# Other seeds for the planner that orders an adaLN transformer block on one core

## The chip, the cores and the metric

One core of one Trainium2 chip runs the whole kernel. The metric is device time in microseconds (us), the median of three runs. Five engines work beside each other: TensorE (PE in the profile, its weight loads PEld), VectorE (DVE), ScalarE (ACT), GpSimd (POOL) and SyncE (SP, which issues nearly all DMAs).

## What is computed

One transformer block of 2048 tokens, 512 channels and 32 heads of 16 channels, with six modulation vectors made from a condition `c`:

```python
x = A_x
mod = (_silu(c) @ w_mod).reshape(c.shape[0], 6, 1, -1)
sa, ca, ga, sb, cb, gb = ...
h = _layernorm(x, axis=-1) * (1 + ca) + sa
x = x + ga * _A_ref(h, A_wqkv, A_wo)        # softmax attention, 32 heads, head width 16
h = _layernorm(x, axis=-1) * (1 + cb) + sb
x = x + gb * _B_ref(h, B_w1, B_b1, B_w2, B_b2)   # 512 -> 1376, gelu, -> 512
return x
```

The softmax over 32 heads of 2048 by 2048 scores is by far the largest part: 134 million exponentials.

## The kernel before

**Tiling.** The queries are cut into four blocks of 512. A run is four heads against one block of queries (in the last block half the queries of eight heads); there are 32 runs, `runs`. A run goes over 16 tiles of 128 keys. A tile of keys is four units of 128 keys by 512 scores, one for each head or half.

**Two ways to take the exponential.** A unit's scores are made by a matmul that uses 32 of the array's 128 rows (`qk`, L824), so that up to four of them run beside each other. On the ACT way (`qk_a`, `ex` at L873) two or three units (`SPAN = (3, 2)`) lie in one PSUM tile `st`, and one ACTIVATE with Exp turns them into `pt`. On the DVE way (`qk_d`, L914, and `shifts`, L929) the score is turned into the bits of a bf16 number by adding a constant (`ph`, four instructions for a tile of keys, one for each unit), and four shifted copies (`sh`, four instructions for a tile of keys) are weighted and averaged. Each product with V (`pv_op`, L962, output `od`) is four matmuls that use all 128 rows: one such group for a tile of keys on the ACT way, five on the DVE way (one with `ph`, four with `sh`). Tiles 2, 6, 10 and 14 of each run (`DKS`; in the first run tile 14 alone) may go either way, up to 31 x 4 + 1 = 125 in all: DVE takes them when it is free for them, and `next_tile` gives those to ACT that DVE has not taken by the time ACT has nothing else of that run.

**Around them** stand the layer norms, the q, k and v projections, the gates (`mod_columns` and `gate_bc`, made after the first and the fourth run), the products with Wo, W1 and W2 for each finished block (`block_tail`), and a tail for the last half block (`last_half`).

**The planner.** All order is fixed when the kernel is built. `Plan` holds a list of work that could be next on each engine and a model of its own of when each engine, tile and buffer is free. `step` asks `pick` for each engine's best candidate and commits the one that starts first. `pick` keeps the candidates that start within a slack of the first and takes the one with the smallest sum of a priority (`dyn`) and `spread`:

```python
def spread(self, o):
    seed = SEEDS[min(int(self.now // 12.5), len(SEEDS) - 1)]
    x = (o.seq * 2654435761 ^ seed * 2246822519) & 0xFFFFFFFF
    x = ((x ^ x >> 15) * 2246822519) & 0xFFFFFFFF
    return SPREAD * (seed % 4) * ((x ^ x >> 13) & 1023) / 1024.0
```

So each stretch of 12.5 us of plan time has a seed. The seed makes a number between 0 and 1 out of each piece of work's serial number, and its remainder by 4 sets how far that number can move a choice: nothing for 0, up to 0.3, 0.6 or 0.9 for 1, 2 and 3 (`SPREAD = 0.3`). The priorities that it is added to lie 0.05 to some units apart: a candidate in PE's present mode has 0.5 less, a second score matmul for an ACT that is already supplied costs 2.2, for a DVE 7.

The planner also keeps a record of PE work (`done`), in which a matmul that uses a part of the rows counts for that part, and holds it against two bounds, `FILL` (1.6 us) and `HEAT` (1.3 us) within `WIN` (3.4 us): work that can wait is held back while the record is full enough, and where it runs short, `heat` adds matmuls on zeros (L433, L438, L449) or doubles a `pv` (`o.extra`, L953). A piece of `mod_columns` (`mod_mm`, four matmuls with one column each, L585, and for every second piece one on zeros, L588) is put down there with 0.36 us.

Of the kernel before, what the change touches and what calls it, by code (L numbers as in the profile page):

```python
# [59 lines left out]
AL = 0.21  # L60
FILL = 1.6
SPREAD = 0.3
SEEDS = (0, 0, 755, 57, 694, 691, 918, 614, 162, 803, 681, 731, 49, 608, 441, 365, 202, 75, 571, 0, 661, 578, 62, 537, 834, 873, 727, 838, 707, 887, 118, 138, 118, 945, 551, 781, 821, 803, 995, 659, 439, 0, 251, 929, 855, 38, 992, 86, 978, 926, 309, 0, 0, 16, 0, 0, 829, 892, 0, 736, 454, 0, 0, 0, 0, 0)
HEAT = 1.3


# [39 lines left out]
class Plan:  # L106
# [51 lines left out]
# [5 lines that stand above are left out]
# [1292 lines left out]
```

## Time and profile before

| | us |
|---|---|
| median of three runs (lowest, highest) | 792.81 (791.49, 794.11) |
| the profiled execution's own time | 788.26 |
| its span, first to last instruction | 786.5 |
| ScalarE's 631 exponentials, busy | 715.7 |
| PE busy on scores for ACT, and for DVE | 249.3, 162.8 |

The mean granted TensorE clock of the profiled execution is 0.991. Busy times are sums over the whole span; for one engine they cover overlapping instructions once. PE's busy time counts waits inside its pipeline, so it is not array use.

The two halves of the page's second part that matter are the rows by slices of the span: the clock row is 9, full speed, in every slice but the seventh, where it is 7.

### The profile page before, as it was taken

To read this page: it belongs to the slowest core of one execution; us is meant where nothing else is said; L and a number is where in the kernel's file an instruction comes from. 1 tells how busy PE (TensorE), PEld (TensorE's weight loads), DVE (VectorE), ACT (ScalarE), POOL (GpSimd) and SP (SyncE) were. 2 spreads that over 40 slices of the span, in tenths; PEclk is the share of its full clock that TensorE was granted. 3 is DMA by queue.
4 is the path that set the end of the run, shared out by engine and by line. 5 is a ranking of instruction groups with operands and counts; after the bars stand their busy time and mean duration, and the time that the engine had idled before them with its cause. 6 is when DMAs were issued, how large, how long until landed. Compare 5 with 4: busy or idle time off the path is not lost.

```text
span 786.5 us, 20298 instructions
## 1 busy us (share of the span) xinstructions
PE 736.1 (94%) x8240; PEld 272.4 (35%) x8240; DVE 732.9 (93%) x1277; ACT 757.6 (96%) x685; POOL 127.9 (16%) x279
## 2 busy tenths in 40 slices
PE   8899989999999888999999999989999999999998
PEld 3333322233332222223323232222233444344454
DVE  6879797999999999999999999998999999999994
ACT  4999998999999999999999999999999999999994
POOL 6520304103224310110001000010000200010100
PEclk9999997999999999999999999999999999999999
DMA  7033001000020101000101100011011001100010
GB/s 215 30 98 129 18 24 43 25 6 17 23 73 24 25 16 50 19 15 13 42 20 29 30 18 17 20 26 39 23 45 29 18 18 26 37 24 18 25 44 28
DMA packets 39072, 28.21 MB, mean 36 GB/s; under 512 B 17957, under 2 KB 34374, under 8 KB 38978
## 3 DMA queue, kind: packets, MB, share of 16 engines
q1 hardware_dynamic: 38970, 26.91, 12.3%
q8 instruction: 64, 1.05, 0.6%
q14 instruction: 30, 0.25, 0.1%
q10 hardware_dynamic: 8, 0.00, 0.0%
HBM read 21.30 MB, written 2.61 MB: 30 GB/s over the span
## 4 chain that ended last, share of the span: by engine, by line
ACT 51%; PE 24%; issue 11%; DVE 10%; DMA 2%; SPq 1%; POOL 1%; POOLq 0%; ACTq 0%; DVEq 0%
ACT pt L873 49%; PE od L962 8%; PE st L824 7%; DVE ph L914 3%; DVE sh L929 2%; PE ax L824 2%; PE ax L1125 2%; DVE ln_s L609 1%; DMA dc<-dn 1%; ACT g L1204 1%; PE ax L1185 1%; PE ax L703 1%; PE ax L433 1%; DMA Wo<-in_A_wo_dram 1%; PE t L1125 1%
## 5 line engine op out<-in xcount | busy, mean ns | idle before, releaser
L873 ACT ACTIVATE pt<-st 128x1536 bf16<-128x1536 f32 (+1 forms) x631 | 715.7, 1351 | 6.1 <-PE st L824 4.0
L914 DVE TENSOR_SCALAR ph<-ax 128x512 int16<-128x512 f32 x472 | 309.7, 681 | 15.2 <-PE ax L824 12.8
L929 DVE TENSOR_SCALAR sh<-ph 128x2048 int16<-128x2048 int16 x472 | 310.7, 691 | 3.3 <-PE od L962 2.7
L824 PE MATMUL st<-qm,kT 32*128 32x512 bf16 x1576 | 249.3, 385 | 28.5 <-ACT pt L873 23.1
L962 PE MATMUL od<-sh,VX 128*32 128x512 bf16 (+1 forms) x2384 | 169.8, 341 | 5.1 <-DVE sh L929 4.5
L824 PEld LDWEIGHTS <-kT 32*128 32x128 bf16 x2048 | 84.0, 91 | 245.6 <-issue 235.5
L824 PE MATMUL ax<-qm,kT 32*128 32x512 bf16 x472 | 162.8, 382 | 4.2 <-DVE ph L914 2.3
L962 PE MATMUL od<-pt,VEB 128*32 128x512 bf16 (+1 forms) x1964 | 150.1, 343 | 0.4 <-DVE OD L987 0.2
L962 PEld LDWEIGHTS <-VEB 128*32 128x32 bf16 x2560 | 62.3, 96 | 79.0 <-issue 66.8
L962 PEld LDWEIGHTS <-VX 128*32 128x32 bf16 x2384 | 59.4, 95 | 77.3 <-issue 66.6
L1014 POOL TENSOR_TENSOR OT<-OD,RB 128x256 bf16<-128x256 f32 x38 | 27.8, 742 | 289.5 <-DVE sh L929 155.8
L962 PE MATMUL od<-ph,VEB 128*32 128x512 bf16 (+1 forms) x596 | 45.8, 338 | 0.3 <-DVE OD L987 0.2
L1014 POOL TENSOR_TENSOR OS<-OD,RB 128x256 bf16<-128x256 f32 x24 | 17.3, 728 | 171.2 <-DVE sh L929 123.7
L1185 PE MATMUL ax<-blk,W 128*128 128x512 bf16 (+1 forms) x164 | 42.7, 362 | 0.3
L703 PE MATMUL ax<-blk,w 128*128 128x512 bf16 x124 | 36.6, 382 | 1.8 <-DVE blk L628 1.5
L758 POOL TENSOR_SCALAR VX<-VEB 128x128 bf16<-128x128 bf16 x64 | 24.6, 386 | 52.7 <-DVE VEB L635 49.3
L1125 PE MATMUL ax<-w,g 128*128 128x512 bf16 x112 | 30.7, 381 | 0.8 <-DVE ph L914 0.6
L1195 DVE TENSOR_SCALAR g<-ax,b1c 128x512 bf16<-128x512 f32 (+1 forms) x41 | 28.1, 689 | 0.5 <-PE ax L1185 0.4
L609 DVE BATCH_NORM_STATS2 ln_s<-xb 128x6 f32<-128x512 bf16 x32 | 21.7, 678 | 1.6 <-DMA xb<-in_A_x_dram 1.5
L1125 PEld LDWEIGHTS <-g 128*128 128x128 bf16 x176 | 14.3, 97 | 22.8 <-issue 11.6
L987 DVE COPY OD<-od 128x512 f32<-128x512 f32 x31 | 21.1, 682 | 0.9 <-PE od L962 0.4
L1185 PEld LDWEIGHTS <-W 128*128 128x128 bf16 x176 | 13.4, 97 | 22.0 <-issue 16.6
(110 smaller groups left out, 371.4 us busy)
## 6 DMA issues: line engine op xcount, KB each, us to landing
RB<-rn SPq DMA_DIRECT2D x124, 64.0 KB
xb<-in_A_x_dram SPq DMA_DIRECT2D x8, 512.0 KB
out_dram<-o SPq DMA_DIRECT2D x16, 128.0 KB
qm<-qs SPq DMA_DIRECT2D x120, 16.0 KB
W<-in_B_w_dram SPq DMA_DIRECT2D x1, 1376.0 KB
w<-in_A_wqkv_dram SPq DMA_DIRECT2D x3, 384.0 KB
blk<-in_w_mod_dram SPq DMA_DIRECT2D x2, 512.0 KB
g<-in_w_mod_dram SPq DMA_DIRECT2D x2, 512.0 KB
```

Of the source, the lines that this page charges most:

```text
L609: nc.vector.bn_stats(out=st6, in_=src)
L703: return chain([(lambda ps, j=j: nc.tensor.matmul(out=ps[:, 0:QB], lhsT=w.tile[:, j, cc * P:(cc + 1) * P], rhs=o_h[b].tile[:, j, :], start ...
L758: nc.gpsimd.tensor_scalar(out=v_cols(VX[(t, ph)])[:, 8 * cc:8 * cc + 8, 0:16], in0=v_cols(v_tile(t, 0))[:, 8 * cc:8 * cc + 8, 0:16], scala ...
L824: nc.tensor.matmul(out=o.tile[:, k * QB:(k + 1) * QB], lhsT=kT[cc][kb][rows, ko * P:(ko + 1) * P], rhs=qm.tile[rows, par, :] if hb is None ...
L873: nc.scalar.activation(out=e.tile[:, 0:len(got) * QB], in_=o.tile[:, 0:len(got) * QB], func=ACT.Exp, scale=ESC)
L914: nc.vector.tensor_scalar(out=ph.tile[:, o.row * QB:(o.row + 1) * QB], in0=o.tile, scalar1=PH_B, scalar2=0.0, op0=ALU.add, op1=ALU.max)
L929: sh = op("DVE", lambda o, j=j: nc.vector.tensor_scalar(out=o.tile, in0=first.tile, scalar1=PH_SH[j], scalar2=None, op0=ALU.add), 0.6, es, ...
L962: nc.tensor.matmul(out=o_od[r].tile[32 * i:32 * i + 32, n * HB:n * HB + w], lhsT=v_tile(kt, ph)[:, c0:c0 + 32], rhs=got[i][:, at:at + w], ...
L1014: two = beside(lambda c: nc.gpsimd.tensor_tensor(out=OT.tile[:, c], in0=OD.tile[:, c], in1=o5.tile[:, c], op=ALU.mult), (OT,), (OD, o5))
L1125: nc.tensor.matmul(out=ps, lhsT=g[:, f, col:col + P], rhs=rhs, start=(f == 0), stop=(f == NF - 1))
L1185: mm = chain([(lambda ps, f=f, j=j: nc.tensor.matmul(out=ps[:, 0:N], lhsT=W1[:, j, f * P:(f + 1) * P], rhs=h.tile[:, j, 0:N], start=(j == ...
L1195: ev.append(op("DVE", lambda o, f=f, mm=mm: nc.vector.tensor_scalar(out=g.tile[:, f, 0:N], in0=mm.tile[:, 0:N], scalar1=b1c[:, f:f + 1], s ...
```

## The change

One constant, the tuple of 66 seeds. Its first three entries, and so the plan up to 37.5 us of plan time, are the same.

```diff
-SEEDS = (0, 0, 755, 57, 694, 691, 918, 614, 162, 803, 681, 731, 49, 608, 441, 365, 202, 75, 571, 0, 661, 578, 62, 537, 834, 873, 727, 838, 707, 887, 118, 138, 118, 945, 551, 781, 821, 803, 995, 659, 439, 0, 251, 929, 855, 38, 992, 86, 978, 926, 309, 0, 0, 16, 0, 0, 829, 892, 0, 736, 454, 0, 0, 0, 0, 0)
+SEEDS = (0, 0, 755, 5, 531, 719, 518, 847, 0, 618, 302, 387, 314, 297, 323, 63, 661, 775, 827, 615, 0, 331, 0, 619, 409, 891, 627, 607, 511, 251, 875, 267, 66, 589, 745, 78, 323, 767, 603, 547, 399, 0, 59, 231, 254, 891, 299, 903, 259, 790, 0, 0, 957, 0, 0, 140, 0, 0, 0, 928, 0, 0, 0, 0, 0, 0)
```

In words, the new seeds were chosen with a penalty on short stretches of the plan that hold little TensorE work. The penalty was used in choosing them and is not in the kernel. Of the old seeds 19, 14, 17 and 16 have the remainders 0, 1, 2 and 3 by 4; of the new ones 21, 7, 8 and 30. No operation, tile, buffer or shape is edited; which engine takes a tile of `DKS`, and how many matmuls on zeros are added, follow from the plan and may differ.

## The prediction

> **What bounds the kernel now.** I read the page first: busy times, the chain of waits, the costliest groups.
>
> ```profile
> span 786.5 us, 20298 instructions
> ...
> PE 736.1 (94%) x8240; PEld 272.4 (35%) x8240; DVE 732.9 (93%) x1277; ACT 757.6 (96%) x685; POOL 127.9 (16%) x279
> ...
> ACT 51%; PE 24%; issue 11%; DVE 10%; DMA 2%; SPq 1%; POOL 1%; POOLq 0%; ACTq 0%; DVEq 0%
> ...
> L873 ACT ACTIVATE pt<-st 128x1536 bf16<-128x1536 f32 (+1 forms) x631 | 715.7, 1351 | 6.1 <-PE st L824 4.0
> L914 DVE TENSOR_SCALAR ph<-ax 128x512 int16<-128x512 f32 x472 | 309.7, 681 | 15.2 <-PE ax L824 12.8
> L929 DVE TENSOR_SCALAR sh<-ph 128x2048 int16<-128x2048 int16 x472 | 310.7, 691 | 3.3 <-PE od L962 2.7
> ```
>
> ACT is busiest and half of the chain is its exponentials, though DVE and PE are close. The 472 `ph` are 118 tiles of keys on the DVE way (four units each), of 125 that may go there; the other 2048 - 472 = 1576 units are ACT's, at 715.7 / 1576 = 0.454 us each.
>
> Then the busy times by stretch, cut where ACT's exponentials become continuous (41.53) and where they end (763.45). After the time in the stretch, the columns are PE, PEld, DVE, ACT and POOL busy with their instruction counts, granted clock, DMA share, GB/s.
>
> ```profile
> 0.00:41.53 41.53, 35.35 (x296) 16.78 (x296) 29.44 (x70) 28.61 (x31) 24.12 (x105) 1.00 0.39 117
> 41.53:763.45 721.92, 681.58 (x7781) 243.95 (x7779) 692.99 (x1183) 717.15 (x623) 102.21 (x170) 0.99 0.12 32
> 763.45:786.50 23.05, 19.13 (x167) 11.62 (x166) 10.43 (x24) 11.86 (x32) 1.60 (x4) 1.00 0.08 25
> ```
>
> In the middle ACT idles for 721.92 - 717.15 = 4.77 us. So an order can win there by two things alone: those 4.77 us, and a different number of units for ACT. ACT's order of time says where the idle lies (start, length, group; idle before it in brackets):
>
> ```profile
> 129.98 2.54 ACT L873 ACTIVATE pt<-st 128x1024 bf16<-128x1024 f32 x2 [0.87 <-PE ax L824]
> 132.68 1.02 ACT L873 ACTIVATE pt<-st 128x1024 bf16<-128x1024 f32 x1 [0.16 <-PE st L824]
> 134.20 1.45 ACT L873 ACTIVATE pt<-st 128x1536 bf16<-128x1536 f32 x1 [0.50 <-PE st L824]
> 136.47 4.62 ACT L873 ACTIVATE pt<-st 128x1024 bf16<-128x1024 f32 x4 [0.82 <-PE ax L824]
> ...
> 264.03 55.61 ACT L873 ACTIVATE pt<-st 128x1024 bf16<-128x1024 f32 x49 [0.84 <-PE st L824]
> 320.67 10.49 ACT L873 ACTIVATE pt<-st 128x1536 bf16<-128x1536 f32 x9 [1.03 <-PE st L824]
> ```
>
> 2.35 us between 129 and 137, 0.84 us at 263, 1.03 us at 320. All wait for scores from PE. Last, short stretches around these places, same columns:
>
> ```profile
> 122.51:125.93 3.42, 2.55 (x32) 1.08 (x28) 3.39 (x7) 3.42 (x4) 1.52 (x3) 1.00 0.29 87
> 125.93:136.17 10.24, 9.91 (x71) 2.55 (x70) 6.63 (x16) 8.13 (x7) 4.26 (x6) 0.50 0.10 28
> 313.66:317.07 3.41, 2.58 (x27) 0.73 (x23) 3.41 (x7) 3.41 (x4) 1.24 (x2) 1.00 0.02 4
> 317.07:320.49 3.42, 3.42 (x25) 0.61 (x24) 2.22 (x4) 2.57 (x3) 0.17 (x1) 0.50 0.08 18
> 259.05:262.46 3.41, 2.60 (x29) 0.75 (x26) 2.15 (x6) 3.41 (x4) 0.82 (x2) 1.00 0.09 16
> 511.60:515.01 3.41, 2.67 (x36) 0.90 (x28) 3.11 (x7) 3.41 (x4) 0.00 (x0) 1.00 0.08 17
> ```
>
> From 125.93 to 136.17 and from 317.07 to 320.49 the granted clock is 0.50: two falls, 10.24 and 3.41 us long and 191.15 us apart, which are 3, 1 and 56.0 times 3.413. So I cut the middle into pieces of 3.413 us on that grid. The two pieces just ahead of the falls are the two in which PE was busy least, 2.55 and 2.58 us; the next, at 259.05, has 2.60 and no fall follows. While the clock is down PE cannot feed both ways and ACT waits 2.35 + 1.03 = 3.38 us.
>
> [...]
>
> **The change part by part.** *Start.* Three seeds stay, so the plan to 37.5 us is the same: 0.
>
> *The falls.* If no piece of the middle is as poor in PE work as those two, ACT gets back 2.35 + 1.03 = 3.38 us. Bounds: nothing, if the poor stretches move instead of going, and 3.38 us; another execution may cut the stretches elsewhere, and 4.55 us lie between the profiled execution's 788.26 and the median 792.81, two to four falls at 1.03 to 2.35 us each. Whether they are falls this profile cannot say, so they only widen the range downward. I take 3.38 us, since what it needs is small: 2.65 us of PE work per piece in place of 2.55. The gap at 263 follows a DVE that waited for a transfer; I leave it.
>
> *The split between ACT and DVE.* A tile moved from DVE to ACT costs ACT 4 x 0.454 = 1.82 us and frees DVE of 4 x 0.681 + 4 x 0.691 = 5.49 us; moved the other way it gives the same. In the middle DVE idles for 721.92 - 692.99 = 28.9 us, room for 5.3 tiles, within the 7 that it leaves to ACT: at best 5.3 x 1.82 = 9.6 us less. On the other side, an order that doubles DVE's idle time loses as much, 9.6 us. No row says which way, so I take 0.
>
> *Matmuls on zeros.* L433, L438, L449 and L953 together are 9.4 + 4.4 + 8.8 + 3.2 = 25.8 us of PE's busy time. A plan with fewer poor stretches may want fewer; one that adds as many again would still lie in PE's 721.92 - 681.58 = 40.3 us of idle middle. Taken 0. If that cover is gone where ACT needs scores, it shows as ACT waiting for `st`, at 0.2 to 1 us a place as above.
>
> *DMAs and the end.* Each DMA is issued as before; those of the normalisation (`RB`, `dn`, `dc`) and of `qm` change places on SP. POOL, which waits for them, is 16% busy; what is late next is `od` after `OD`, and PE waited 0.2 us for that. Behind the last exponential lie 23.05 us in which seeds are 0 in both plans but for one (454 to 0): 0, with 1 us either way.
>
> *Sum.* Against the profiled execution: 786.5 - 3.4 = 783.1 of span, 788.26 - 3.38 = 784.9 of time. Its own time lies 4.55 us under the median of the runs shown, so the same step from the median gives 792.81 - 3.38 = **789.4 us**.
>
> [...]
>
> **The rivals.**
>
> *Fewer tiles for DVE.* Seeds that spread PE work evenly are not those that give ACT least work. For it: 30 of the new seeds against 16 have the remainder that moves choices most, by up to 0.9, which outweighs the 0.5 that keeps PE in its mode; and DVE's largest wait is already for scores (12.8 us for `ax`). Against it: the same disorder may fill DVE's 28.9 idle us. Four tiles fewer make 4 x 1.82 = 7.3 us, less 3.38: 792.81 + 3.9 = 796.7. Where the falls go, it makes the kernel slower beyond 0.3% from (3.38 + 2.38) / 1.82 = 3.2 tiles; where they stay, from 1.3 tiles.
>
> *More tiles for DVE.* Two: 789.4 - 3.6 = 785.8.
>
> *The planner does not see the first fall.* The piece ahead of it holds the columns of `mod_mm`:
>
> ```profile
> L585 PE MATMUL ax<-sc,g 128*128 128x1 bf16 x32 | 1.8, 168 | 0.0
> L588 PE MATMUL ax<-warm 128*128 128x384 bf16 x4 | 1.8, 442 | 0.0
> ```
>
> The planner puts eight pieces down at 0.36 us, 2.9 us of PE work; the L585 rows hold 1.8 us for 32 columns of one element. A penalty on the planner's account finds nothing poor there. Then the second fall alone goes: 792.81 - 1.03 = 791.8. Against it: any other order shifts what stands beside those columns.
>
> *Falls have nothing to do with these orders.* 2.58 fell and 2.60 did not, which is thin. Then nothing changes: 792.8.
>
> **How the numbers follow.** A measurement of this kernel can tell about 0.3% from no change, 2.4 us: 790.4 and 795.2 are the bounds. Chances: falls gone with the split about as it was 0.34 (789.4; own range 787 to 790.4), more tiles for DVE 0.10, first fall unseen 0.18, nothing to do with it 0.05, fewer tiles or new falls of its own 0.33. So faster 0.34 + 0.10 = 0.44, same 0.18 + 0.05 = 0.23, slower 0.33. The range runs from 784.5, which holds two tiles more and leaves out most of the four-fall gain, to 797.5, four tiles fewer and a little; one in ten is left outside at each end.
>
> **What would show it.** Right: granted clock 1.00 in every stretch between 41 and 763, ACT idle there under 1.5 us, `ph` 472 give or take 4, span near 783. Wrong by the split: `ph` at 456 or fewer and more than 631 exponentials. Wrong by the planner's account: a fall still at the columns of L585 after the first run. Wrong altogether: as many falls as before, at other places, or ACT waiting for `st` at full clock.

## The result and the profile after

| | us, median | runs (lowest to highest) |
|---|---|---|
| before: the three runs shown with the prediction and two more | 792.81 | 5 (791.49 to 794.11) |
| changed | 786.26 | 5 (784.57 to 788.06) |
| before, three later jobs together | 789.71 | 93 (784.37 to 797.17) |
| changed, two of those jobs | 787.64 and 787.05 | 12 and 12 (784.48 to 789.12) |

The first comparison gives a ratio of 0.9918 (95% interval 0.9894 to 0.9942), the two repeats 0.997 (0.9945 to 0.9996) and 0.996 (0.9936 to 0.9984). The kernel is faster in all three, though the interval of the first repeat ends just under 1. How much faster was a question of its own, since the first five runs of before lay high: 28 of the 93 later ones reach 791.49.

The page of the changed kernel, the same lines as before:

```profile
span 786.2 us, 20185 instructions
...
PE 727.6 (93%) x8136; PEld 274.3 (35%) x8215; DVE 732.8 (93%) x1277; ACT 757.6 (96%) x685; POOL 128.4 (16%) x279
...
ACT 45%; PE 28%; DVE 13%; issue 10%; DMA 2%; POOL 1%; SPq 0%; POOLq 0%; DVEq 0%; ACTq 0%
...
L873 ACT ACTIVATE pt<-st 128x1536 bf16<-128x1536 f32 (+1 forms) x631 | 715.5, 1364 | 5.5 <-PE st L824 4.6
L914 DVE TENSOR_SCALAR ph<-ax 128x512 int16<-128x512 f32 x472 | 309.5, 681 | 13.4 <-PE ax L824 11.5
L929 DVE TENSOR_SCALAR sh<-ph 128x2048 int16<-128x2048 int16 x472 | 311.4, 690 | 1.7 <-PE od L962 1.1
```

The split between ACT and DVE is the same to the instruction: 631 exponentials, 472 `ph`, 472 `sh`, and the busy times agree within 1 us. The span of this execution, 786.2, is within 0.3 us of the profiled one of before, 786.5. So the page alone would say that nothing happened. (PE's 8136 matmuls against 8240 are mostly records that the trace lacks: L703 has 95 of 124 here, and 124 in a later profile of the changed kernel. The rest is a difference of the plans: L449, groups of four matmuls on zeros, has 64 in place of 88.)

Where the profiled execution lost time, by stretches. Columns as in the prediction: PE, PEld, DVE, ACT and POOL busy, granted clock, DMA share, GB/s. The last line is a piece that no fall follows.

```profile
31.47:34.88 3.41, 2.39 (x18) 0.98 (x17) 2.62 (x3) 2.89 (x5) 2.09 (x18) 1.00 0.00 0
34.88:41.71 6.83, 6.47 (x41) 3.05 (x40) 2.96 (x6) 4.91 (x4) 0.29 (x1) 0.50 0.07 17
304.53:307.94 3.41, 2.36 (x28) 0.73 (x28) 3.41 (x7) 3.41 (x4) 0.00 (x0) 1.00 0.27 55
307.95:311.36 3.41, 3.41 (x30) 0.70 (x23) 2.40 (x4) 2.78 (x3) 0.67 (x1) 0.50 0.13 32
...
615.13:618.55 3.42, 2.26 (x42) 1.19 (x42) 2.82 (x6) 3.42 (x4) 2.17 (x2) 1.00 0.00 0
```

The two falls at 126 and 317 us are gone, and two others are there: 6.83 us at 34.88, in a part of the program that both kernels share, and 3.41 us at 307.95. ACT's order of time shows where it idles for them (idle before each group in brackets):

```profile
34.84 1.02 ACT L873 ACTIVATE pt<-st 128x1024 bf16<-128x1024 f32 x1 [0.52 <-PE st L824]
36.18 1.45 ACT L873 ACTIVATE pt<-st 128x1536 bf16<-128x1536 f32 x1 [0.32 <-PE st L824]
37.81 1.02 ACT L873 ACTIVATE pt<-st 128x1024 bf16<-128x1024 f32 x1 [0.17 <-PE st L824]
39.74 1.45 ACT L873 ACTIVATE pt<-st 128x1536 bf16<-128x1536 f32 x1 [0.91 <-PE st L824]
42.02 1.02 ACT L873 ACTIVATE pt<-st 128x1024 bf16<-128x1024 f32 x1 [0.82 <-PE st L824]
...
43.40 3.73 ACT L873 ACTIVATE pt<-st 128x1536 bf16<-128x1536 f32 x3
...
310.28 1.02 ACT L873 ACTIVATE pt<-st 128x1024 bf16<-128x1024 f32 x1 [0.57 <-PE st L824]
311.70 97.28 ACT L873 ACTIVATE pt<-st 128x1536 bf16<-128x1536 f32 x86 [0.40 <-PE ax L824]
```

2.74 us around the early fall, 0.97 us around the other. The first 0.52 us of the 2.74 are not the fall's. A later profile of the changed kernel, which has no early fall, shows them too:

```profile
35.68 5.54 ACT L873 ACTIVATE pt<-st 128x1024 bf16<-128x1024 f32 x5 [0.52 <-PE st L824]
...
41.53 4.70 ACT L873 ACTIVATE pt<-st 128x1536 bf16<-128x1536 f32 x4
```

From the first of these five exponentials to the one behind them ACT takes 43.40 - 34.84 = 8.56 us with the fall and 41.53 - 35.68 = 5.85 us without it. So the early fall costs 2.7 us. Idle time alone gives 2.2, since exponentials that do not wait overlap a little: the five have 5.96 us of their own and take 5.54 together.

The same kernel falls near 35 us in one execution and not in another, so one profile of each kernel is one draw. Every run lists its span and mean granted clock, and those are what to compare.

### The profile page after: what moved, and what is told of

It reads as the page before. It is cut to its first block, busy times and chain, and to the rows that moved or that the text cites. A ratio compares the mean times of both kernels' runs of the same rounds, so it can differ in the third digit from the quotient of the medians.

```text
span 786.2 us, 20185 instructions
## 1 busy us (share of the span) xinstructions
PE 727.6 (93%) x8136; PEld 274.3 (35%) x8215; DVE 732.8 (93%) x1277; ACT 757.6 (96%) x685; POOL 128.4 (16%) x279
## 4 chain that ended last, share of the span: by engine, by line
ACT 45%; PE 28%; DVE 13%; issue 10%; DMA 2%; POOL 1%; SPq 0%; POOLq 0%; DVEq 0%; ACTq 0%
ACT pt L873 43%; PE od L962 9%; PE st L824 8%; DVE sh L929 5%; DVE ph L914 4%; PE ax L824 2%; PE ax L1185 2%; PE ax L1125 2%; ACT g L1204 1%; DVE ln_s L609 1%; PE ax L703 1%; DMA blk<-in_w_mod_dram 1%; PE t L1125 1%; PE ax L742 1%; PE ax L1119 1%
## 5 line engine op out<-in xcount | busy, mean ns | idle before, releaser
L873 ACT ACTIVATE pt<-st 128x1536 bf16<-128x1536 f32 (+1 forms) x631 | 715.5, 1364 | 5.5 <-PE st L824 4.6
L824 PE MATMUL st<-qm,kT 32*128 32x512 bf16 x1576 | 248.4, 384 | 34.4 <-ACT pt L873 27.7
L962 PE MATMUL od<-sh,VX 128*32 128x512 bf16 (+1 forms) x2384 | 173.9, 341 | 4.0 <-DVE sh L929 2.7
L824 PEld LDWEIGHTS <-kT 32*128 32x128 bf16 x2048 | 84.2, 91 | 241.2 <-issue 231.9
L824 PE MATMUL ax<-qm,kT 32*128 32x512 bf16 x472 | 163.9, 379 | 3.9 <-DVE ph L914 2.2
L962 PE MATMUL od<-pt,VEB 128*32 128x512 bf16 (+1 forms) x1964 | 151.0, 342 | 0.1
L962 PEld LDWEIGHTS <-VEB 128*32 128x32 bf16 x2560 | 63.0, 95 | 80.2 <-issue 68.7
L962 PEld LDWEIGHTS <-VX 128*32 128x32 bf16 x2384 | 61.0, 95 | 78.3 <-issue 67.2
L962 PE MATMUL od<-ph,VEB 128*32 128x512 bf16 (+1 forms) x596 | 47.0, 338 | 0.1
L1185 PE MATMUL ax<-blk,W 128*128 128x512 bf16 (+1 forms) x144 | 39.1, 359 | 1.8 <-issue 1.0
L703 PE MATMUL ax<-blk,w 128*128 128x512 bf16 x95 | 30.7, 388 | 3.2 <-DVE blk L628 1.5
L1125 PE MATMUL ax<-w,g 128*128 128x512 bf16 x102 | 28.8, 381 | 0.8 <-issue 0.3
L742 PE MATMUL ax<-w,blk 128*128 128x128 bf16 x256 | 21.1, 226 | 0.2 <-DVE ph L914 0.2
```

What stands on the lines that cost most here:

```text
L703: return chain([(lambda ps, j=j: nc.tensor.matmul(out=ps[:, 0:QB], lhsT=w.tile[:, j, cc * P:(cc + 1) * P], rhs=o_h[b].tile[:, j, :], start ...
L742: nc.tensor.matmul(out=ps[:, t * P:(t + 1) * P], lhsT=o_h[b].tile[:, j, t * P:(t + 1) * P], rhs=o_w[2].tile[:, j, cc * P:(cc + 1) * P], st ...
L824: nc.tensor.matmul(out=o.tile[:, k * QB:(k + 1) * QB], lhsT=kT[cc][kb][rows, ko * P:(ko + 1) * P], rhs=qm.tile[rows, par, :] if hb is None ...
L873: nc.scalar.activation(out=e.tile[:, 0:len(got) * QB], in_=o.tile[:, 0:len(got) * QB], func=ACT.Exp, scale=ESC)
L962: nc.tensor.matmul(out=o_od[r].tile[32 * i:32 * i + 32, n * HB:n * HB + w], lhsT=v_tile(kt, ph)[:, c0:c0 + 32], rhs=got[i][:, at:at + w], ...
L1125: nc.tensor.matmul(out=ps, lhsT=g[:, f, col:col + P], rhs=rhs, start=(f == 0), stop=(f == NF - 1))
```

## The experiments

Theory 1: the gain is fewer falls of the clock. Theory 2: the new order is shorter by itself. All runs were timed against before in the same job.

**The changed kernel again, and its clock.** No edit.

> The changed kernel once more, beside runs of the kernel before, for span against granted clock. Theory 1 (the gain is falls of the clock that no longer happen): both kernels lie on one line; executions at a clock of 1.000 span 782 to 784 us, and each 0.01 of mean clock lost adds about 4 us, so that the kernel before, at 788 to 793, has clocks of 0.975 to 0.99. Theory 2 (the new order is shorter by itself): at the same mean clock the kernel before is 4 us or more longer than the changed one.

Median 787.64. The runs of both kernels, side by side at nearly the same clock, with the number of executions in brackets (17 of the changed kernel, its first 5 and the 12 of this job, and the 35 of before in this job):

```
mean granted clock   span before                  span changed
1.000                783.0 (1)                    782.7, 782.8 (2)
0.997 to 0.995       784.1, 784.9 (2)             783.6 to 786.1 (6)
0.993                785.0, 785.5 (2)             786.2 to 787.3 (7)
0.991                785.5 to 786.4 (8)           -
0.987 to 0.984       787.9 to 790.2 (11)          -
0.983 to 0.972       791.0 to 794.5 (9)           -
```

(Two of each kernel, at 0.989 and at 0.998, are left out.) At full clock both kernels take 783 us, and at 0.993 the changed one is 1 to 2 us longer. So theory 2 is wrong: what differs is how low the clock goes. In the profile shown with the prediction and in the one shown with the result the granted clock is 0.50 in the falls and, in the second, in the last 0.4 us; everywhere else it is 1.00. So the time that an execution spends at half clock follows from its mean clock: (1 - clock) x 2 x span. For those two that gives 14.2 and 11.0 us, where the falls add up to 13.65 and 10.24. A line through all 93 runs of before gives span = 782.1 + 0.309 x that time, and through the changed kernel's 29, with a slope of 0.309 as well, 783.2. The mean time at half clock is 20.2 us before (93 runs) and 6.9 us after (29 runs).

**The changed kernel, second time, on the chip of the last job.**

> The changed kernel on the same chip as the run above, as its control: mean low-clock time 6 to 8 us, 786.5 to 787.5 if the earlier runs tell the whole; 785 to 786 if they were an unlucky draw. Against the kernel before a ratio of 0.996 (theory 1, 3 us by falls), not 0.992.

787.05, ratio 0.996, mean time at half clock 6.8 us: as theory 1 had it.

**The kernel before, another look.** No edit, one execution.

> [...] Theory 1: again a fall between 116 and 135 us, at the modulation columns, and the others at other places than 317 us; span 783 plus 0.3 us for each us at half clock.

```profile
123.14:126.55 3.41, 2.73 (x35) 1.46 (x35) 3.41 (x11) 3.41 (x4) 1.39 (x3) 1.00 0.06 10
126.55:129.97 3.42, 3.24 (x28) 0.88 (x27) 2.26 (x5) 2.54 (x4) 2.45 (x3) 0.50 0.32 81
594.18:597.59 3.41, 2.90 (x30) 0.81 (x27) 3.41 (x7) 3.41 (x4) 0.73 (x1) 1.00 0.06 14
597.59:601.01 3.42, 3.42 (x20) 0.83 (x19) 2.24 (x4) 2.66 (x3) 0.00 (x0) 0.50 0.08 20
...
259.67:263.08 3.41, 2.13 (x29) 0.65 (x28) 2.98 (x6) 2.47 (x4) 0.00 (x0) 1.00 0.11 11
```

A fall at the modulation columns again, and one at a new place, 597.59, as expected; span 784.8, two falls of 3.41 us, and 782.1 + 0.309 x 6.8 = 784.2. The pieces ahead of these falls have PE busy for 2.73 and 2.90 us, more than several pieces of the same execution that no fall follows; the last line shows one, with 2.13 us.

**Four matmuls at the columns, order of before.**

```diff
-        if m % 2 and warmer:
+        if warmer:
```

> The kernel before with a matmul on zeros after each piece of the modulation columns instead of every second (four more, in the stretch of the first fall, nothing else). Theory 1, with the planner blind to how little work these columns are: one fall of 7 to 10 us fewer in most executions, 1.5 to 2.5 us less than before, 790 to 791.5. Theory 2: 792 to 793.

787.11 against 790.52, ratio 0.9953 (0.9928 to 0.9977): 3.4 us from four matmuls on zeros, more than the 1.5 to 2.5 us that theory 1 expected, and level with the whole change in the same job (787.64). Mean time at half clock 8.6 us in place of 20.2. With the order kept, this place alone cost the kernel before some 12 us at half clock in a mean execution.

**The same four, in the changed kernel.** Same edit.

> The changed kernel with a matmul on zeros after each piece of the modulation columns (four more). Theory 1a (the new order took that fall away by putting products with V between the columns): nothing left to win there, mean low-clock time 5 to 8 us as in the changed kernel, 786 to 788. Theory 1b (the falls that went are others, and the columns still fall in many executions): 2 to 4 us less, as with the kernel before.

784.87, ratio 0.9945 (0.9917 to 0.9972), time at half clock 1.7 us. Theory 1b, not 1a: the changed kernel still falls there in some executions. One of its later profiles shows it:

```profile
126.47:129.89 3.42, 2.72 (x38) 1.37 (x30) 3.42 (x11) 3.42 (x4) 2.36 (x4) 1.00 0.12 26
129.89:133.30 3.41, 3.41 (x27) 0.72 (x28) 1.22 (x4) 2.65 (x3) 2.19 (x3) 0.50 0.21 60
```

A likely reason why they are fewer than before stands in PE's order of time around the columns (L585): first the kernel before, from the prediction's profile, then the changed one, from the profile shown with the result.

```profile
123.62 0.40 PE L962 MATMUL od<-pt,VEB 128*32 128x512 bf16 x4
123.95 0.35 PE L585 MATMUL ax<-sc,g 128*128 128x1 bf16 x8
...
125.10 0.25 PE L585 MATMUL ax<-sc,g 128*128 128x1 bf16 x4
...
125.88 0.26 PE L585 MATMUL ax<-sc,g 128*128 128x1 bf16 x4
...
126.27 0.29 PE L585 MATMUL ax<-sc,g 128*128 128x1 bf16 x4
```

```profile
122.14 0.35 PE L585 MATMUL ax<-sc,g 128*128 128x1 bf16 x8
...
123.06 0.40 PE L962 MATMUL od<-pt,VEB 128*32 128x512 bf16 x4
123.33 0.40 PE L962 MATMUL od<-sh,VX 128*32 128x512 bf16 x4
123.55 0.40 PE L962 MATMUL od<-ph,VEB 128*32 128x512 bf16 x4
...
124.40 0.35 PE L585 MATMUL ax<-sc,g 128*128 128x1 bf16 x8
...
125.32 0.61 PE L962 MATMUL od<-sh,VX 128*32 128x512 bf16 x8
125.76 0.39 PE L962 MATMUL od<-pt,VEB 128*32 128x512 bf16 x4
...
128.10 0.25 PE L585 MATMUL ax<-sc,g 128*128 128x1 bf16 x4
...
128.92 0.25 PE L585 MATMUL ax<-sc,g 128*128 128x1 bf16 x4
...
129.20 0.24 PE L585 MATMUL ax<-sc,g 128*128 128x1 bf16 x4
...
130.03 0.25 PE L585 MATMUL ax<-sc,g 128*128 128x1 bf16 x4
```

Before, the first five pieces (four matmuls each; a line with x8 holds two) follow each other with only score matmuls and matmuls on zeros between them. After, groups of products with V (L962) stand between and behind the first two pairs. The last four pieces, at 128 to 130 us, still have no such group between them, and the fall of the later profile begins just behind them. That the products are the reason is read from these two orders; no run moved them alone.

The two runs with four matmuls also say how much of the change is not at the columns. Without that place the order of before has 8.6 us at half clock left, the new order 1.7 (2.8 in the next run). So of the 13.3 us at half clock that the change saves (20.2 less 6.9), about half lies elsewhere; no run tells which places these are.

**Once more, since eight of twelve executions at a clock of 0.999 or 1.000 seemed too many.**

> The changed kernel with four more matmuls on zeros at the modulation columns, once more, since eight executions of twelve at full clock are more than that place alone explains: the fall near 35 us comes before the columns and cannot depend on them. If the columns are the reason: mean low-clock time under 3 us again and 785 to 785.5. [...]

785.22, ratio 0.9943 (0.992 to 0.9965), time at half clock 2.8 us, seven of twelve at full clock and two at 0.993. So the gain holds: 24 runs with a mean of 785.5 against 787.1 for the changed kernel's 29. In its profile ACT's exponentials run from 42 to 407 us, up to the gelu, without a gap:

```profile
42.24 364.45 ACT L873 ACTIVATE pt<-st 128x1536 bf16<-128x1536 f32 x322
```

Why the early fall, which comes ahead of the columns, should be rarer in this kernel is not explained; it may be the draw.

**Filling wherever the plan is poor.** The planner gets a second record, `real`, in which a piece of the columns counts for 0.12 us in place of 0.36. Where the last 3.4 us of it hold less than `POOR`, a product with V gets up to three groups of four matmuls on zeros, which the plan's own times do not count:

```diff
+            self.real.append((s, 0.12 if o.us == 0.36 else self.done[-1][1]))
+            while self.real[0][0] < s - WIN:
+                self.real.popleft()
+            if o.kind == "pv" and o.last_left() > 1:
+                us = o.us / (2 if o.extra else 1)
+                while o.extra < 3 and sum(x for _, x in self.real) < POOR:
+                    o.extra += 1
+                    self.real.append((s, us))
...
-            if o.extra:
+            for _ in range(o.extra):
                 zeros(r)
```

with `POOR = 1.8` (us).

> The seeds and the plan of before, with up to three groups of matmuls on zeros behind a product with V wherever the plan's last 3.4 us hold under 1.8 us of PE work (51 groups more, not counted in the plan). Theory 1: the falls go, the clock is 0.997 or more and the time 784 to 787.5, level with the changed kernel although the order is that of before. Theory 2: 790 to 796, the old order and up to 51 x 0.22 = 11 us of PE work on top.

> The changed kernel with the same filling (47 groups more). Theory 1: the falls that the changed kernel still has go as well: clock 0.999 or more, 783.5 to 785.5, 1 to 2.5 us under the changed kernel, and less spread between runs. Theory 2: 786 to 790, no gain and some PE work on top.

792.26 (ratio 1.0028, 0.9996 to 1.0059) and 790.41 (1.0007, 0.9979 to 1.0035): both miss theory 1's range, and the first lies in theory 2's. Not for its reason, though: by lines through their runs the two filled kernels take 786.7 and 786.3 at full clock, so the orders are equally long once more. The time at half clock fell, from 20.2 to 13.6 us with the old order, but hardly in the new one (6.9 to 6.1), and the work itself costs: the two executions of the changed kernel filled at full clock take 785.8 and 786.3, 3.3 us more than 782.7 and 782.8. The row of the added groups, in the old order (the line is L449 in the kernel before):

```profile
L459 PE MATMUL od<-warm 128*32 128x512 bf16 x292 | 26.6, 391 | 0.0
```

292 against 88 before, 51 groups of four. Theory 2's 11 us of added PE work was not paid either: 786.7 against 782.1 is 4.6 us, some 90 ns for each group (some 70 ns in the new order, 3.3 us for 47). Two profiles without a fall show where a part of it goes: ACT's waits between 41 and 762 us in the changed kernel filled (its L883 and L834 are L873 and L824), then in the changed kernel with the four matmuls at the columns.

```profile
ACT pt L883 <- PE st L834: 1.4, 4, 0.7
ACT pt L883 <- PE ax L834: 0.7, 3, 0.3
...
ACT pt L873 <- PE st L824: 0.3, 1, 0.3
```

ACT waits for scores seven times, 2.1 us in all, against once, 0.3 us.

**Filling the early fall.** At first two matmuls on zeros ahead of the first transposes of each half in the layer norms of the second and third block of tokens, together with the four at the columns.

> The seeds and order of before, the four matmuls on zeros at the columns, and two ahead of the first transposes of each half in the second and third layer norm (eight more), where PE waits for DVE and two profiles show a fall near 35 us. Theory 1: 783.5 to 786 with a clock of 0.995 or more, at or under the changed kernel with the order of before. Theory 2 (orders differ by more than falls): above the changed kernel's 786 to 788.

> The changed kernel with both additions. Theory 1: the fall near 35 us, at 2.7 us a time in perhaps half of its executions, goes: clock 0.997 or more, 784 to 786, 1 to 2 us less than the changed kernel. Theory 2: 786 to 788.

787.91 (0.998, 0.9955 to 1.0005) and 788.34 (0.9976, 0.9952 to 1.0001): both miss theory 1's range, there is no gain over the columns alone (787.11 and 784.87), and both profiles still show a fall near 37 us. The place was wrong: PE's wait near 35 us (0.93 us for DVE's `z`, L620, in the profile of the changed kernel) belongs to the layer norm of the fourth block. So there instead, in the changed kernel and with the columns:

> The kernel of the first run with matmuls on zeros at the transposes of the fourth layer norm, where PE waits 0.9 us for DVE near 35 us (the earlier addition stood at the second and third layer norm, 6 to 14 us ahead of that place). Theory 1: no fall near 35 us in any execution, clock 0.998 or more nearly throughout, 784.3 to 785.2, spread under 1 us. Theory 2: no difference to the first run, or the added work delays the start by 0.5 us or more.

787.01, ratio 0.9956 (0.9936 to 0.9976), time at half clock 5.5 us, so theory 1 misses again. It is 1.8 us slower than the columns alone in the same job. Its one profile has no early fall, but one of 6.8 us at 631. Two executions at a clock of 0.999 have spans of 783.6 and 784.6. Whether the early fall is gone stays open; the addition doesn't pay.

**Seeds that meet another plan.** The new seeds for entries 0 to 12, the old ones behind them.

> The new seeds up to 162.5 us of plan time and the old ones behind them, so that the later ones meet a plan that they were not chosen for. If the prediction's price for the split is right (1.82 us for each tile of keys that moves from DVE to ACT), with 113 tiles on the DVE way in place of 118 the time at full clock is 9 to 10 us longer: 792 to 797. If only falls count and the split does not, 784 to 790.

```profile
L873 ACT ACTIVATE pt<-st 128x1536 bf16<-128x1536 f32 x639 | 725.0, 1352 | 12.0 <-PE st L824 7.7
L914 DVE TENSOR_SCALAR ph<-ax 128x512 int16<-128x512 f32 x452 | 296.1, 683 | 34.4 <-PE ax L824 32.2
```

802.72, ratio 1.0163 (1.0127 to 1.0198), six runs, over both expected ranges. 452 `ph`, five tiles fewer for DVE; ACT's exponentials are busy 9.3 us longer, 1.86 us for each tile, as the prediction priced it. The rest of the 13 us over before is not in falls: the mean time at half clock is 16.0 us, less than the 20.2 of before, and with the slope of 0.309 the span at full clock is 795.6, 13.5 us over 782.1. So some 4 us at full clock are something else. The rows show longer waits for scores, ACT's (12.0 us idle before its exponentials against 6.1, a part of it in the profile's four falls) and DVE's (32.2 us against 12.8); how the 4 us divide is not shown.

## Why the prediction was right, point by point

- **What bounds.** Right: ACT is all but continuous in both kernels (busy for 717.15 and 719.53 of the middle's 721.92 us), the split did not move, and the two kernels take the same 783 us when the clock stays up.
- **The falls, 3.38 us.** The mechanism holds: the gain is time at half clock. The size came out near, but not by the two falls that it was read from. The mean time at half clock went from 20.2 to 6.9 us; at 0.309 us each that is 4.1 us, less 1.1 us that the changed kernel's line lies higher (783.2 against 782.1): 3.0 us, as the means of the runs have it (790.1 of before's 93 later ones, 787.1 of the changed kernel's 29). The sum took 2.35 + 1.03 us from one execution of before that had 13.65 us at half clock, fewer than the mean, and supposed that no fall would be left. The two errors nearly cancel, which is luck.
- **792.81 as the start.** The forecast, 789.4, is 3.1 us above the 786.26 measured first. The step from one median to the next was 6.55 us there and 2.9 and 2.5 us in the repeats. The 4.55 us between the profiled execution and the median were put down as "two to four falls", perhaps; a mean execution has two falls of 3.41 us more than the profiled one, 2.0 us at the slope above. Five runs that all lie in the upper 30% are unlikely if each run draws its falls afresh (0.3 to the fifth power is 0.2%), so something else may bear on that batch. It stays open.
- **What a piece needs, 2.65 us of PE busy.** Wrong. Falls came after pieces with 2.72, 2.73 and 2.90 us, and pieces with 2.26 us (615.13 in the changed kernel) and 2.13 us (259.67 in the kernel before, looked at again) had none behind them. By this measure the poorest pieces did not even get fuller: the changed kernel's profile has 2.26 and 2.36 us where that of before has 2.55 and 2.58. PE's busy time, with its modelled ends and missing records, sets no border between pieces; what does is open.
- **Its own signs.** Of the four signs of being right only the 472 `ph` are in the profiled execution. It has a fall at 307.95, ACT idles in the middle for 721.92 - 719.53 = 2.39 us in place of under 1.5, and its span is 786.2 in place of 783 (one of the first five runs, without a profile, has a clock of 1.000 and a span of 782.8). The sign of being wrong by the planner's account, a fall at the columns, came in a later profile. So the forecast of a gain held, but not the picture of an execution without falls.
- **The split, 1.82 us a tile.** Taken 0, measured 0; the price itself was confirmed at 1.86 us by the mixed seeds. That rival was real for seeds not chosen for the plan they meet.
- **Matmuls on zeros, taken 0.** The change has six groups fewer (L449, 64 against 88), and the two kernels are equally long at full clock. The cover that the prediction gave to added PE work is wrong as a rule: 40.3 us of PE idle in the middle did not hide 51 groups, which cost 4.6 us. It shows where the prediction said that it would if the cover was gone, in ACT waiting for scores (2.1 us against 0.3 at full clock).
- **The planner does not see the columns.** Given as a rival of 0.18, and half true: the falls there became rarer, probably by the products with V between the first columns, but not gone. Four matmuls at the columns win 1.6 us more on the mean.

## What to carry to other kernels

When two executions of one kernel differ by 1%, put span against mean granted clock for all runs before explaining a single profile: here 93 points gave the price of a us at half clock, and showed, with the changed kernel's 29, that two orders are equally long within about 1 us. The falls here were cheaper cured at the one stretch whose work the planner overrates (four matmuls, 3.4 us) than by filling by rule (51 groups, no gain). The fastest version here is the changed order with those four matmuls: 784.87 and 785.22 against 789.71 and 789.56.

## What the hardware showed that was not expected

- The changed kernel falls at 34.88 us, for 6.83 us, in one profiled execution and not there in two others. The two falls of that execution begin a whole number of 3.4133 us (a third of the prediction's 10.24) apart: 307.95 - 34.88 = 273.07 us is 80.0 of them. So do the two of the other look at the kernel before: 597.59 - 126.55 = 471.04 us is 138.0. But where this grid lies changes from run to run: the falls of the changed kernel begin 0.75 us behind a multiple of 3.4133 us from the first instruction in the first profile (34.88 and 307.95), 1.88 us in the second (524.12) and 0.18 us in the third (129.89). One profile could not show that.
- The price of half clock is 0.31 us for each us (the slope through the 93 runs of before), not one half. ACT goes on from the scores that it has: in the fall at 307.95 it is busy for 2.78 of 3.41 us, with PE at half its clock.
- The early fall costs 2.7 us for 6.83 us, 0.40 us for each, more than the mean price of 0.31. One execution shows it; why is not shown.
